# A recurrence and eight experts on one core: the second weight halves of the first two experts wait for gathered rows, and the row-number work is moved

## The chip, the cores and the metric

The kernel runs on one core of a Trainium2 chip. The metric is the device time of one execution in microseconds (us). A core has five engines with instruction streams of their own: TensorE (PE, matmuls), VectorE (DVE), ScalarE (ACT), GpSimd (POOL) and SyncE (SP, which here only issues DMAs). Each stream is executed in its written order, and the streams wait for one another, and for DMAs, on semaphores.

## The reference

A gated recurrence over 4 batches, 8 heads, 768 steps gives the rows x (3072 tokens of 384 numbers). A gate gives 8 logits for each token. Tokens are assigned greedily, by falling logit over all tokens and experts, with room for 384 tokens in each expert. Each expert then puts its 384 rows through two matrices.

```python
for t in range(S):
    state = alpha[:, :, t, :, None] * state + np.einsum('bhd,bhe->bhde', k[:, :, t], v[:, :, t])
    y[:, :, t] = np.einsum('bhd,bhde->bhe', q[:, :, t], state)
...
for idx in np.argsort(-(x @ w_gate).flatten()):
    tok, e = (int(idx) // E, int(idx) % E)
    if assigned[tok] >= 0 or counts[e] >= cap:      # cap = 3072 // 8 = 384
        continue
    assigned[tok] = e; counts[e] += 1
...
for e in range(E):
    mask = assigned == e
    out[mask] = np.maximum(x[mask] @ w1[e], 0.0) @ w2[e]   # w1[e]: 384 x 1024, w2[e]: 1024 x 384
```

## The kernel before

**First part (to about 140 us).** The recurrence is computed in chunks of 128 steps, ordered by a planner of its own. Its rows go to `x_dram`, its logits stay on the chip. The change does not touch it.

**Second part.** The experts are taken in the order in which they fill up. "Expert 0" is the first to be full, "expert 7" the last; which weights that means is known only when the search for it has ended. For every expert i the program has these steps:

- `search(i)` finds, in five rounds over the digits of the logits (`compare` on DVE, small counting matmuls `rt` on PE), which expert fills next. It ends with the number `ei` and calls `weights(i, ei)`: SP loads the raw weights `w1r` and `w2r` in two halves each (768 KB a piece). A half is `load_w1(hf)` and `load_w2(hf)`.
- `extract(i)` computes the numbers of the 384 rows: DVE builds `hot` (left operand) and `rhs` (right operand), PE multiplies them into `xt`, DVE turns that into `idx`, and POOL issues three gathers (`xr<-x_dram,idx`, 128 rows each).
- `update(i)` takes the expert's tokens out and starts the next search. It ends with the first, 3072 wide `compare` for expert i+1. It is called ahead of `search(i+1)`.
- `prep(i)`: PE transposes the three blocks of gathered rows, ACT and DVE split them into a high part `xh` and a rest `xl`.
- `split(i, hf)`: each weight half is split the same way. ACT copies the raw half into `w1hi` (rounded) and, negated, into `w1lo`; then a DMA issued by POOL adds the raw half onto the negative ("low-part DMA", `w1lo<-w1r`, `w2lo<-w2r`, function `low`), so that the rest stays. For the first half of expert 0 POOL itself subtracts `w1lo`.
- `ffn1(i, q)`, q = 0 to 7: nine matmuls into `h` (three with `xh,w1hi`, three with `xl,w1hi`, three with `xh,w1lo`); ACT makes `hh` of it and DVE `hl`. There are two `h` buffers, so that `ffn1(i, 2)` has to wait for `hh` and `hl` of `ffn1(i, 0)`.
- `ffn2(i, q)`: nine matmuls with `w2hi` and `w2lo` into the sums `y0`, `y1`, `y2`. It follows `ffn1` two steps later. At the end of an expert ACT evicts `y` to `yt`, and POOL scatters `yt` to the output (`out_dram<-yt,idx`).

Blocks q = 0 to 3 use half 0 of the weights, q = 4 to 7 half 1. There is room for two experts' raw weights.

**What sets the order.** In the second part a scheduler places the instructions of every engine at build time, by priority. The searches and row numbers of the first three experts have the highest (`ROUTE_AHEAD`). `tc.issue_after(x)` puts what is built under it behind instruction x in that order. `tc.add_manual_dep` adds a wait on the landing of a DMA. What stands in a stream is then executed strictly in that order, so that an instruction that waits holds up all that is written behind it on its engine.

The lines of before that matter here are these:

```python
half(0)                                    # L600, in weights(i, ei)
if i:
    half(1)
else:
    load_w1(1)
    second_half.append(load_w2)            # issued by extract(0), after its last gather has landed
```

Of the kernel before, what the change touches and what calls it, by code (L numbers as in the profile page):

```python
# [21 lines left out]
OP = mybir.AluOpType  # L22
# [131 lines left out]
def gla_moe_kernel(ctx, tc, q, k, v, alpha, w_gate, w1, w2, out):  # L154
    nc = tc.nc
# [29 lines left out]
    NB = CAP // 128  # L185
# [363 lines left out]
    for s in range(NS):  # L549
        pl.base = 4.4 * (NS - s)  # L550
        rows = step(s)
# [32 lines left out]
    def weights(i, ei):  # L584
        ev = nc.sync.value_load(ei[0:1, 0:1], min_val=0, max_val=E - 1)
        W1R[i] = wp.tile([128, DB, F], F32, name="w1r")
        W2R[i] = wp.tile([128, FB, Dm], F32, name="w2r")

        def load_w1(hf):
            fs = slice(hf * F // 2, (hf + 1) * F // 2)  # L590
            return nc.sync.dma_start(W1R[i][:, :, fs], w1v[bass.ds(ev, 1), :, :, fs].rearrange("e p c f -> p (e c) f"))

        def load_w2(hf):
            qs = slice(hf * FB // 2, (hf + 1) * FB // 2)
            return nc.sync.dma_start(W2R[i][:, qs], w2v[bass.ds(ev, 1), :, qs].rearrange("e p c d -> p (e c) d"))

        def half(hf):
            return load_w1(hf), load_w2(hf)

        half(0)  # L600
        if i:
            half(1)
        else:
            load_w1(1)
            second_half.append(load_w2)

    def compare(i, d, t):
        nt = 2 ** BITS[t]
# [137 lines left out]
    def update(i):  # L746
# [10 lines left out]
        if i + 2 < E:  # L757
            sg = rw.tile([128, NU], I32, name="sg")
            nc.vector.tensor_scalar(sg, m.bitcast(I32), 31, -2 ** 31, op0=OP.arith_shift_right,  # L759
                                    op1=OP.bitwise_or)  # L760
            nc.vector.scalar_tensor_tensor(asg, sel, es, asg, op0=OP.mult, op1=OP.add)
            key = rw.tile([128, NU], I32, name="key")
            nc.vector.tensor_tensor(key, m.bitcast(I32), sg, op=OP.bitwise_xor)
            val = rw.tile([128, NU, E], BF, name="val")
            nc.vector.tensor_tensor(val, lw, row(m, E), op=OP.is_equal)
            dig = rw.tile([128, nb, NU], BF, name="dig")
            digits(key, dig, rw, NU)
            st["dig"] = dig
            for _ in compare(i + 1, dig[:, 0], 0):
                pass  # L770
        else:
            nc.vector.scalar_tensor_tensor(asg, sel, es, asg, op0=OP.mult, op1=OP.add)
            val = rw.tile([128, NU, E], BF, name="val")
            nc.vector.tensor_tensor(val, lw, row(m, E), op=OP.is_equal)
# [34 lines left out]
    def extract(i):  # L809
# [15 lines left out]
        for a in range(len(halves(i, True))):  # L825
            js = halves(i, True)[a]
            x = nc.vector.tensor_tensor(words(hot, 64, js), keyed(wb, 64, js), each(iota, 64, js), op=OP.is_equal)
            if a == 0:
                nc.vector.tensor_tensor(rhs, bk, cst, op=OP.mult)
        if i < 3:  # L830
            st["hot"] = x
        ix = psx.tile([128, 2, 2, NB], F32, name="xt")
        with ExitStack() as es_:
            if i == 0:
# [13 lines left out]
        if i:  # L848
            XR[i] = wp.tile([128, NB, Dm], F32, name="xr")
        for b in range(NB):  # L850
            last_gather[0] = nc.gpsimd.indirect_dma_start(  # L851
                out=XR[i][:, b], out_offset=None, in_=x_dram,
                in_offset=bass.IndirectOffsetOnAxis(ap=IDX[i][:, b:b + 1], axis=0))

        for half in second_half:
            tc.add_manual_dep(half(1).ins, last_gather[0].ins.name,
                              mybir.DependencyInfo(mybir.DependencyClass.Sync, mybir.DependencyReason.DATA),
                              reason="rows of the first expert before its later weights")
        second_half.clear()

    last_gather = [None]

    XH, XL, CH, XA = {}, {}, {}, {}

    def split(i, hf):
# [10 lines left out]

        def low(x, raw_):
            with ExitStack() as es:
                if i == 0:
                    es.enter_context(tc.issue_after(last_gather[0].ins))  # L880
                return nc.gpsimd.dma_start(x.bitcast(F32), raw_, accum_op=OP.add, max_dma_last_dim=8192)  # L881

# [174 lines left out]
```

## Time and profile before

| | |
|---|---|
| runs | 429.5, 435.35, 435.58 us; median 435.35 us |
| the profiled execution | 426.99 us, its span (first to last instruction) 425.3 us |
| matmuls (PE) busy | 391.8 us, 92% of the span |
| DVE, ACT, POOL busy | 282.3, 214.6, 188.8 us |
| DMA | 88.05 MB, mean 207 GB/s; queue 0 (issued by POOL) 37.9%, queue 1 (issued by SP) 37.2% of 16 engines' span |
| first transpose of expert 0, 1, 2 on PE | 164.38, 196.59, 234.66 us |

Times in the profile are counted from the start of the span. A row of the timeline reads: start, duration, engine, line of the kernel, operation, output<-inputs, shape, count; in brackets follows how long the engine had been idle before it and what ended that. In a row on DMA issues the last number is the time from issue to landing in us. PEclk is the clock granted to PE, 1.00 being full.

### The profile page before, as it was taken

The numbers are of one execution on the slowest core, as the hardware profiler recorded it, in microseconds if no ns is written. First come the engines' busy times: TensorE is split into PE (matmuls) and PEld (weight loads), VectorE is DVE, ScalarE is ACT, GpSimd is POOL, SyncE is SP. The second block draws the span as 40 slices with busy tenths as digits, with TensorE's granted clock in tenths as the row PEclk, the third lists the DMA queues.
The fourth block names the chain that finished last, engine by engine and source line by source line (L and its number), as shares of the span: only waits on it lengthen the run. The fifth ranks groups of instructions, "written<-read, shape, count | busy, mean of one in ns | idle before, by whom it ended". The sixth has DMA issues, their size and how long they took to land.

```text
span 425.3 us, 10054 instructions
## 1 busy us (share of the span) xinstructions
PE 391.8 (92%) x3884; PEld 348.9 (82%) x3884; DVE 282.3 (66%) x861; ACT 214.6 (50%) x381; POOL 188.8 (44%) x206
## 2 busy tenths in 40 slices
PE   4699999999998887998998999999899999999992
PEld 1588899887886445997997898899789999999992
DVE  5999799899983585686587497796887922312210
ACT  1265655664553006526718528528626729659211
POOL 8498777766840006115505325336253342623102
PEclk9799999999999999997999699999999999999998
DMA  8967998863020149599689989998994999999701
GB/s 287 352 203 234 310 327 242 273 195 106 20 76 26 53 143 254 105 246 282 147 208 299 188 232 267 209 276 250 194 325 151 226 257 363 248 290 201 163 0 55
DMA packets 43679, 88.05 MB, mean 207 GB/s; under 512 B 3824, under 2 KB 18160, under 8 KB 43632
## 3 DMA queue, kind: packets, MB, share of 16 engines
q0 software_dynamic: 11376, 33.82, 37.9%
q1 hardware_dynamic: 32256, 53.60, 37.2%
q8 instruction: 30, 0.49, 0.5%
q14 instruction: 17, 0.14, 0.1%
HBM read 53.59 MB, written 9.44 MB: 148 GB/s over the span
## 4 chain that ended last, share of the span: by engine, by line
PE 55%; issue 14%; DVE 13%; DMA 12%; POOL 2%; ACT 1%; SPq 1%; POOLq 0%; DVEq 0%
PE h L946 15%; PE y L966 13%; DMA xr<-x_dram,idx 4%; PE y L444 4%; PE s L393 4%; PE xt L381 4%; PE y L437 4%; DMA w1lo<-w1r 4%; DMA rq<-in_q_dram 2%; PE lg L456 2%; PE rt L666 2%; PE rt L669 2%; DVE te L353 2%; PE xt L930 2%; DVE cmp L614 2%
## 5 line engine op out<-in xcount | busy, mean ns | idle before, releaser
L950 ACT ACTIVATE hh<-h 128x384 fp32r<-128x384 f32 x64 | 31.4, 490 | 94.0 <-PE h L946 93.6
L951 DVE SCALAR_TENSOR_TENSOR hl<-h,hh 128x384 fp32r<-128x384 f32 x64 | 35.4, 554 | 55.4 <-ACT hh L950 55.2
L966 PE MATMUL y<-w2hi,hh 128*128 128x384 f32 x192 | 67.6, 352 | 0.0
L966 PE MATMUL y<-w2lo,hh 128*128 128x384 f32 x192 | 67.2, 350 | 0.0
L966 PE MATMUL y<-w2hi,hl 128*128 128x384 f32 x192 | 66.6, 348 | 0.0
L977 POOL DMA_INDIRECT out_dram<-yt,idx x24 | 27.0, 1127 | 56.4 <-ACT yt L970 52.4
L881 POOL DMA_DIRECT2D w1lo<-w1r x15 | 20.2, 1346 | 67.5 <-ACT w1lo L893 55.0
L946 PE MATMUL h<-xh,w1hi 128*128 128x384 f32 x192 | 45.9, 343 | 1.7 <-DVE hl L951 1.7
L851 POOL DMA_INDIRECT xr<-x_dram,idx x24 | 29.9, 1247 | 39.3 <-DVE sg L759 18.2
L946 PE MATMUL h<-xh,w1lo 128*128 128x384 f32 x192 | 45.8, 340 | 0.0
L946 PE MATMUL h<-xl,w1hi 128*128 128x384 f32 x192 | 45.1, 339 | 0.0
L893 ACT ACTIVATE w1hi<-w1r 128x768 fp32r<-128x768 f32 x32 | 26.7, 837 | 22.5 <-DVE sg L759 21.9
L966 PEld LDWEIGHTS y<-w2hi,hh 128*128 128x128 f32 x192 | 37.5, 195 | 0.0
L363 POOL TENSOR_TENSOR kh<-rk,te 128x512 f32<-128x512 f32 (+1 forms) x24 | 29.4, 1227 | 18.0 <-DVE z L373 11.5
L966 PEld LDWEIGHTS y<-w2lo,hh 128*128 128x128 f32 x192 | 37.4, 195 | 0.0
L966 PEld LDWEIGHTS y<-w2hi,hl 128*128 128x128 f32 x192 | 37.2, 195 | 0.1
L946 PEld LDWEIGHTS h<-xh,w1hi 128*128 128x128 f32 x192 | 33.8, 189 | 2.3 <-DVE hl L951 2.0
L946 PEld LDWEIGHTS h<-xl,w1hi 128*128 128x128 f32 x192 | 34.0, 188 | 0.5 <-DVE xl L935 0.2
L946 PEld LDWEIGHTS h<-xh,w1lo 128*128 128x128 f32 x192 | 34.1, 188 | 0.0
L614 DVE TENSOR_TENSOR cmp<-nd,iota 128x1536 bf16<-128x1536 bf16 (+3 forms) x32 | 32.7, 1031 | 0.8
L396 POOL TENSOR_SCALAR_AFFINE_SELECT sm<-sm 128x1024 f32<-128x1024 f32 x24 | 26.2, 1093 | 14.1 <-ACT sm L395 12.4
L395 ACT ACTIVATE sm<-s 128x1024 f32<-128x1024 f32 x24 | 24.6, 1025 | 14.5 <-PE s L393 13.6
(182 smaller groups left out, 838.6 us busy)
## 6 DMA issues: line engine op xcount, KB each, us to landing
w1r<-in_moe_w_dram SPq DMA_DIRECT2D x16, 768.0 KB, 9.0
w2r<-in_moe_w_dram SPq DMA_DIRECT2D x16, 768.0 KB, 11.5
w2lo<-w2r POOLq DMA_DIRECT2D x16, 768.0 KB, 9.2
w1lo<-w1r POOLq DMA_DIRECT2D x15, 768.0 KB, 7.7
al<-in_alpha_dram SPq DMA_DIRECT2D x24, 260.0 KB, 4.3
rk<-in_k_dram SPq DMA_DIRECT2D x24, 256.0 KB, 4.5
rq<-in_q_dram SPq DMA_DIRECT2D x24, 256.0 KB, 4.3
rv<-in_v_dram SPq DMA_DIRECT2D x24, 192.0 KB, 3.8
```

Of the source, the lines that this page charges most:

```text
L363: eng.tensor_tensor(out_.t[:, us].rearrange("p u c -> p (u c)"), x.t[:, lo:hi], f.t[:, lo:hi], op=OP.mult)
L395: add(A_, 1.05, lambda: nc.scalar.activation(sm.t, sc.t, AF.Copy), r=[(sc, 0), (sc, 1)], w=[sm])
L396: add(G_, 1.15, lambda: nc.gpsimd.affine_select(sm.t, sm.t, pattern=[[0, 8], [1, C]], compare_op=OP.is_ge, fill=0.0, base=0, channel_multi ...
L614: nc.vector.tensor_tensor(words(dst, nt, js), keyed(d, nt, js), each(iotas[t], nt, js), op=OP.is_ge)
L851: last_gather[0] = nc.gpsimd.indirect_dma_start(out=XR[i][:, b], out_offset=None, in_=x_dram, in_offset=bass.IndirectOffsetOnAxis(ap=IDX[i ...
L881: return nc.gpsimd.dma_start(x.bitcast(F32), raw_, accum_op=OP.add, max_dma_last_dim=8192)
L893: nc.scalar.activation(dst, src, AF.Copy, scale=scale)
L946: nc.tensor.matmul(o, a[:, d], x[:, d], start=(n == 0), stop=(n == 3 * DB - 1))
L950: HA[i, q] = nc.scalar.activation(hh, o, AF.Relu)
L951: nc.vector.scalar_tensor_tensor(hl, o, 0.0, hh, op0=OP.max, op1=OP.subtract)
L966: F2[i, q] = nc.tensor.matmul(Y[b], a[:, bs], w, start=(q == 0 and n == 0), stop=(q == FB - 1 and n == 2))
L977: st_ = nc.gpsimd.indirect_dma_start(out=out, out_offset=bass.IndirectOffsetOnAxis(ap=IDX[i][:, b:b + 1], axis=0), in_=yt, in_offset=None)
```

## The change

Three things are changed. First, the second half of `w1` of expert 0, and both second halves of expert 1, are issued from `extract`, each with a wait on the landing of a gather: `w1` of expert 0 on the first of its three gathers, the others on the last. (The second half of `w2` of expert 0 waited for the last gather already.) Second, for experts 1 and 2 `rhs` is built right behind `hot` and ahead of `update`, whose start is tied to `rhs` instead of `hot`; the first `compare` for expert 3 is put behind the row numbers `idx` of expert 2. Third, the low-part DMAs of the first halves of experts 1 and 2 are put behind the gathers of that expert, as those of expert 0 are.

```diff
@@ weights
         half(0)
-        if i:
+        if i > 1:
             half(1)
         else:
-            load_w1(1)
-            second_half.append(load_w2)
+            second_half.extend((load_w1, load_w2))
@@ update
             st["dig"] = dig
-            for _ in compare(i + 1, dig[:, 0], 0):
-                pass
+            with tc.issue_after(st["idx"].ins) if i == 2 else ExitStack():
+                for _ in compare(i + 1, dig[:, 0], 0):
+                    pass
@@ extract
             if a == 0:
-                nc.vector.tensor_tensor(rhs, bk, cst, op=OP.mult)
+                with tc.issue_after(x.ins):
+                    y = nc.vector.tensor_tensor(rhs, bk, cst, op=OP.mult)
         if i < 3:
-            st["hot"] = x
+            st["hot"] = x if i == 0 else y
...
-            last_gather[0] = nc.gpsimd.indirect_dma_start(
+            gathers[b] = last_gather[0] = nc.gpsimd.indirect_dma_start(
...
-        for half in second_half:
-            tc.add_manual_dep(half(1).ins, last_gather[0].ins.name,
+        for n, load_ in enumerate(second_half):
+            tc.add_manual_dep(load_(1).ins, gathers[0 if n == i == 0 else NB - 1].ins.name,
@@ split, low
-                if i == 0:
+                if i == 0 or i < 3 and not hf:
                     es.enter_context(tc.issue_after(last_gather[0].ins))
```

Line numbers of the changed kernel differ from those of before by one in places (L966 of before is L967).

The first place is SyncE's stream around the loads of expert 1 (`w1r_2600`, `w2r_2601`; the value loaded before them is `ei`). The rows of before:

```order
L585 TENSOR_LOAD ei_2455 [waits DVE_49]
L585 ISA x2
L591 ISA
L591 DMA w1r_2600<-in_moe_w1_dram 128x3x512
L595 ISA
L595 DMA w2r_2601<-in_moe_w2_dram 128x4x384
L591 ISA
L591 DMA w1r_2600<-in_moe_w1_dram 128x3x512
L595 ISA
L595 DMA w2r_2601<-in_moe_w2_dram 128x4x384
```

In the changed kernel the second `w1r` has a wait on a DMA that POOL issued (`DMASW0`, the last gather of expert 1):

```order
L591 DMA w1r_2600<-in_moe_w1_dram 128x3x512
L595 ISA
L595 DMA w2r_2601<-in_moe_w2_dram 128x4x384
L591 ISA
L591 DMA w1r_2600<-in_moe_w1_dram 128x3x512 [waits DMASW0_49]
L595 ISA
L595 DMA w2r_2601<-in_moe_w2_dram 128x4x384
```

No row has moved; the second `w1r` waits, and with it the second `w2r` behind it. In the loads of expert 0 the second `w1r` has gained such a wait too.

The second place is ScalarE's stream where expert 1 begins. `xh_2666` are its rows, `w1hi_2804` and `w1lo_2805` its half 1, `w2lo_2807` the same of `w2`, `hh_2710` and `hh_2733` belong to `ffn1(1, 0)` and `ffn1(1, 1)`; `yt_2740` and `yt_2745` are evictions of expert 0. Before:

```order
L893 ACTIVATE w1hi_2804<-w1r_2600 128x3x256 [waits DMAHW6_49,Pool_49]
L933 ACTIVATE xh_2666<-xt_2680 128x3x128 [waits PE_49]
L970 ACTIVATE yt_2740<-y0_2279 128x384 [waits PE_49]
L970 ACTIVATE yt_2745<-y1_2280 128x384 [waits PE_49]
L893 ACTIVATE w1lo_2805<-w1r_2600 128x3x256
L893 ACTIVATE w1hi_2804<-w1r_2600 128x3x256
L893 ACTIVATE w1lo_2805<-w1r_2600 128x3x256
L950 ACTIVATE hh_2710<-h_2700 128x384 [waits DVE_49,PE_49]
L893 ACTIVATE w2lo_2807<-w2r_2601 128x768 [waits DMAHW7_49,DMASW3_49]
L950 ACTIVATE hh_2733<-h_2723 128x384 [waits DVE_49,PE_49]
```

In the changed kernel:

```order
L934 ACTIVATE xh_2666<-xt_2680 128x3x128 [waits PE_49]
L894 ACTIVATE w1hi_2804<-w1r_2600 128x3x256 [waits DMAHW6_49,Pool_49]
L971 ACTIVATE yt_2740<-y0_2279 128x384 [waits PE_49]
L894 ACTIVATE w1lo_2805<-w1r_2600 128x3x256
L894 ACTIVATE w1hi_2804<-w1r_2600 128x3x256
L894 ACTIVATE w1lo_2805<-w1r_2600 128x3x256
L951 ACTIVATE hh_2710<-h_2700 128x384 [waits DVE_49,PE_49]
L894 ACTIVATE w2lo_2807<-w2r_2601 128x768 [waits DMAHW7_49,DMASW3_49]
L951 ACTIVATE hh_2733<-h_2723 128x384 [waits DVE_49,PE_49]
```

`w1hi_2804`, which waits for the second `w1r` (`DMAHW6`), has moved behind `xh`, one eviction has moved behind `hh_2733`; `hh_2710` still stands behind the copies of half 1.

The third place is the row numbers of expert 2, on VectorE and then on GpSimd. Before, VectorE's rows (`cmp0_100` is the compare for expert 3, `other` and `idx` are the last steps to the row numbers):

```order
L782 TENSOR_TENSOR chu_3424<-ch_3421,un_3419 128x24
L783 SCALAR_TENSOR_TENSOR rem_90<-cl_3102,rem_90 128x8
L614 TENSOR_TENSOR cmp0_100<-dig_3412,iota_73 128x3072
L785 TENSOR_TENSOR o_3427<-ramp_b_75,chu_3424 128x192
L829 TENSOR_TENSOR rhs_3131<-bk_3128,cst_87 128x144
L951 SCALAR_TENSOR_TENSOR hl_2852<-h_2841,hh_2851 128x384
L676 TENSOR_TENSOR gt0_96<-rt_3431,rem_90 128x8
L842 TENSOR_SCALAR other_3148<-xt_3134 64x3
```

In the changed kernel `rhs_3131` stands 17 rows further up, right behind `hot`, and this place reads:

```order
L783 SCALAR_TENSOR_TENSOR rem_90<-cl_3102,rem_90 128x8
L843 TENSOR_SCALAR other_3148<-xt_3134 64x3
L785 TENSOR_TENSOR o_3427<-ramp_b_75,chu_3424 128x192
L844 TENSOR_SCALAR other_3148<-xt_3134 64x3
L845 TENSOR_TENSOR idx_3147<-xt_3134,other_3148 64x3
L846 TENSOR_TENSOR idx_3147<-xt_3134,other_3148 64x3
L613 TENSOR_TENSOR cmp0_100<-dig_3412,iota_73 128x3072
L952 SCALAR_TENSOR_TENSOR hl_2852<-h_2841,hh_2851 128x384
```

The four steps to `idx` now stand ahead of the compare and of one `hl`. GpSimd's rows of the same place, before (`w1lo_2805` and `w2lo_2807` are half 1 of expert 1, `w1lo_3178` and `w2lo_3180` half 0 of expert 2, `xr_3153` its gathers):

```order
L881 DMA w1lo_2805<-w1r_2600 128x3x512
L977 DMA out_0_dram<-yt_2750,idx_2152 3072x384
L881 DMA w2lo_2807<-w2r_2601 128x1536
L881 DMA w1lo_3178<-w1r_3088 128x3x512
L851 DMA xr_3153<-x_dram_62,idx_3147 128x384 x3
L881 DMA w2lo_3180<-w2r_3089 128x1536
```

In the changed kernel:

```order
L882 DMA w1lo_2805<-w1r_2600 128x3x512
L978 DMA out_0_dram<-yt_2745,idx_2151 3072x384
L978 DMA out_0_dram<-yt_2750,idx_2151 3072x384
L882 DMA w2lo_2807<-w2r_2601 128x1536
L852 DMA xr_3153<-x_dram_62,idx_3147 128x384 x3
L882 DMA w1lo_3178<-w1r_3088 128x3x512
L882 DMA w2lo_3180<-w2r_3089 128x1536
```

`w1lo_3178` has moved behind the three gathers.

More of the change, by code (lines that the diff above doesn't have):

```diff
@@ L850, in extract @@
         for b in range(NB):
-            last_gather[0] = nc.gpsimd.indirect_dma_start(
+            gathers[b] = last_gather[0] = nc.gpsimd.indirect_dma_start(
                 out=XR[i][:, b], out_offset=None, in_=x_dram,
                 in_offset=bass.IndirectOffsetOnAxis(ap=IDX[i][:, b:b + 1], axis=0))
-        for half in second_half:
-            tc.add_manual_dep(half(1).ins, last_gather[0].ins.name,
+        for n, load_ in enumerate(second_half):
+            tc.add_manual_dep(load_(1).ins, gathers[0 if n == i == 0 else NB - 1].ins.name,
                               mybir.DependencyInfo(mybir.DependencyClass.Sync, mybir.DependencyReason.DATA),
-                              reason="rows of the first expert before its later weights")
+                              reason="rows of the first experts before their later weights")
         second_half.clear()
-    last_gather = [None]
+    last_gather, gathers = [None], {}
     XH, XL, CH, XA = {}, {}, {}, {}
```

## Prediction

> **What bounds the kernel now.** I read the slices of the span first, then the second part in windows.
>
> ```profile
> PE   4699999999998887998998999999899999999992
> PEclk9799999999999999997999699999999999999998
> DMA  8967998863020149599689989998994999999701
> ```
>
> A slice is 10.6 us. PE is busy nine tenths nearly everywhere, so the time is that of PE's stream, and only what makes PE wait or run slowly can be won. Its clock drops twice in the second part, in slices 19 and 23. DMA is near its full share from slice 16 to 37, with one half empty slice (31).
>
> ```profile
> 164.00:168.00 4.00, 3.62 (x44) 3.04 (x44) 1.12 (x3) 2.42 (x5) 3.50 (x4) 1.00 1.06 184
> 196.00:205.00 9.00, 7.98 (x42) 7.15 (x42) 3.56 (x6) 4.38 (x8) 1.78 (x3) 0.62 0.99 192
> 233.00:243.00 10.00, 8.34 (x51) 7.54 (x52) 4.27 (x11) 5.27 (x9) 3.56 (x4) 0.66 0.93 197
> ```
>
> The third number from the right is the granted clock. It costs 9 x (1 - 0.62) = 3.4 us at the start of expert 1 and 10 x (1 - 0.66) = 3.4 us at that of expert 2. PE's timeline tells what it had waited for:
>
> ```profile
> 164.38 0.52 PE L930 MATMUL xt<-ident,xr 128*128 128x128 f32 x3 [3.04 <-DMA xr<-x_dram,idx]
> 166.69 0.49 PE L930 MATMUL xt<-ident,xr 128*128 128x128 f32 x3
> 196.59 0.90 PE L930 MATMUL xt<-ident,xr 128*128 128x128 f32 x3 [1.42 <-DMA xr<-x_dram,idx]
> 197.92 0.87 PE L930 MATMUL xt<-ident,xr 128*128 128x128 f32 x3 [0.43 <-DMA xr<-x_dram,idx]
> 234.66 0.90 PE L930 MATMUL xt<-ident,xr 128*128 128x128 f32 x3 [2.53 <-DMA xr<-x_dram,idx]
> ```
>
> Experts 0, 1 and 2 wait for gathered rows, 3.04, 1.85 and 2.53 us. The first wait brought no slow clock (1.00 in 164 to 168), the other two did. So there are 3.04 + (1.85 + 3.4) + (2.53 + 3.4) = 14.2 us at which the change can aim, 3.3% of the 426.99 us of the profiled execution.
>
> **Expert 0: the second `w1` half behind the first gather.** From issue to landing, in this order: that half (issued at 155.30), the first gather (158.55), the third gather of expert 2 (232.28), the quickest in this part, and the second `w2` half of expert 0 (165.25), which went beside one low-part DMA.
>
> ```profile
> w1r<-in_moe_w_dram SPq DMA_DIRECT2D x1, 768.0 KB, 8.4
> xr<-x_dram,idx POOLq DMA_INDIRECT x1, 5.7
> xr<-x_dram,idx POOLq DMA_INDIRECT x1, 3.3
> w2r<-in_moe_w_dram SPq DMA_DIRECT2D x1, 768.0 KB, 6.3
> 158.55 1.18 POOL L851 DMA_INDIRECT xr<-x_dram,idx  x1 [18.20 <-DVE sg L759]
> 161.31 1.04 POOL L851 DMA_INDIRECT xr<-x_dram,idx  x1 [0.30 <-issue]
> 167.60 0.84 ACT L893 ACTIVATE w1hi<-w1r 128x768 fp32r<-128x768 f32 x1
> 170.10 0.49 ACT L950 ACTIVATE hh<-h 128x384 fp32r<-128x384 f32 x1 [0.93 <-PE h L946]
> ```
>
> The first gather landed at 164.25, half a microsecond behind the 8.4 us load. With that load held back it should come at 158.55 + 3.3 = 161.9, the third at 161.31 + 3.3 = 164.6; PE took the third block at 166.69, so up to 2.0 us are there. The held load is then issued at 161.9 and, at 6.3 us, lands at 168.2. But its first copy, `w1hi`, stood at 167.60 on ACT, ahead of `hh` of `ffn1(0, 0)` at 170.10. From the start of that copy to `hh` ACT needs two copies (0.74 and 0.84 us apart), so `hh` starts at 169.8, only 0.3 us earlier than before, though PE is ready at 168.1. Since the two `h` buffers let one more `ffn1` run meanwhile, a part of the 2.0 us stays. I take **-1.0 us**. Bounds: -2.0 (load at 4.5 us, as the very first `w1r` alone), +1.9 (load at 8.4 us again: `hh` at 171.9). Nothing else is queued behind the waiting load on SP but the `w2` half, which waited for the third gather already.
>
> **Expert 1: both second halves behind the third gather.** These are rows of before; the DMA rows are the held `w1r` (issued 185.75), then three other `w1r` loads that went beside two low-part DMAs (issued 276.19, 328.55 and 302.32).
>
> ```profile
> w1r<-in_moe_w_dram SPq DMA_DIRECT2D x1, 768.0 KB, 9.2
> w1r<-in_moe_w_dram SPq DMA_DIRECT2D x1, 768.0 KB, 8.8
> w1r<-in_moe_w_dram SPq DMA_DIRECT2D x1, 768.0 KB, 9.8
> w1r<-in_moe_w_dram SPq DMA_DIRECT2D x1, 768.0 KB, 12.2
> w1r<-in_moe_w_dram SPq DMA_DIRECT2D x1, 768.0 KB, 4.5
> 185.75 0.43 SPq L591 DMA_DIRECT2D w1r<-in_moe_w_dram  x1
> 192.51 2.20 POOL L851 DMA_INDIRECT xr<-x_dram,idx  x1 [0.30 <-issue]
> 194.71 1.43 POOL L881 DMA_DIRECT2D w1lo<-w1r  x1
> 195.68 1.41 POOL L881 DMA_DIRECT2D w2lo<-w2r  x1
> 199.95 0.83 ACT L893 ACTIVATE w1hi<-w1r 128x768 fp32r<-128x768 f32 x1
> 204.44 0.84 ACT L893 ACTIVATE w1lo<-w1r 128x768 fp32r<-128x768 f32 x1
> 207.02 0.49 ACT L950 ACTIVATE hh<-h 128x384 fp32r<-128x384 f32 x1 [0.28 <-PE h L946]
> 203.85 0.88 PE L946 MATMUL h<-xh,w1hi 128*128 128x384 f32 x4
> 209.12 0.34 PE L946 MATMUL h<-xh,w1hi 128*128 128x384 f32 x1
> ```
>
> (The fifth is that first `w1r` of all, issued at 153.77 with nothing beside it.) *What is removed:* the gathers no longer run against four loads. They should land before PE asks, so the 1.85 us wait and the 3.4 us of slow clock go. PE would reach `ffn1(1, 2)`, at 209.12 before, at 209.12 - 1.85 - 3.4 + 0.5 (three `ffn2` matmuls that now stand ahead of it, 0.17 us each) - 1.0 (expert 0) = 203.4.
>
> *What is late instead:* the held load. The third gather took 2.20 us on POOL, ended at 194.71, and should land 2.4 us behind that end (the 3.3 us gather took 0.95 us to issue), which with the 1.0 us of expert 0 gives 196.1. Only then is `w1r` issued, beside the two low-part DMAs of half 0 that left POOL 1 to 2 us earlier. The rows of such company are 8.8, 9.8 and 12.2 us; I take 9.3, so it lands at 205.4, ten microseconds later than the 194.9 of before. ACT's `w1hi` of half 1 waits for it, and behind it in ACT's stream stand an eviction, three more copies, and `hh` of `ffn1(1, 0)`. From the landing to that `hh` it takes 0.74 + 0.39 + (207.02 - 204.44 - 0.3 of idle) = 3.4 us; `hl` on DVE is done 1.1 us later. `ffn1(1, 2)` needs that buffer, so it starts at 205.4 + 4.5 = 209.9: **+0.8 us** against before, after PE has stood still for 209.9 - 203.4 = 6.5 us. Bounds by the 4.5 and 12.2 us rows: 205.1 (-4.0) and 212.8 (+3.7). The second `w2` half lands some 3 us later, for copies that stand behind `hh`.
>
> A stall like this will bring the slow clock back, since waits of 1.85 and 2.53 us have done so: at most 3.4 us, of which a part may pass while PE still stands. I take **+3.0 us** (0 to 3.4).
>
> Here a rule bears on the price. The Trainium skill, page "TensorE: Matmul & The Clock Gate", section "HAM oscillation — how this bites in real kernels", wants no idle gap of PE above about 3.4 us. By the page a stall of 6.5 us cools the clock and one of 3 us need not; the trace does not bear out the limit, for 1.85 us cooled and 3.04 did not. By the page the sum for a stall below 3.4 us would be 3.0 us better, at 6.5 us it is the same.
>
> **Expert 2: row numbers earlier, low-part DMA behind the gathers.**
>
> ```profile
> 221.10 0.95 DVE L827 TENSOR_TENSOR hot<-wb,iota 128x1536 f16<-128x1536 bf16 x1
> 224.25 1.75 DVE L614 TENSOR_TENSOR cmp<-dig,iota 128x3072 bf16<-128x3072 bf16 x1
> 226.19 0.23 DVE L829 TENSOR_TENSOR rhs<-bk,cst 128x144 f16<-128x144 f16 x1
> 228.41 0.17 DVE L845 TENSOR_TENSOR idx<-xt,other 64x3 int32<-64x3 f32 x1
> 226.51 1.29 POOL L881 DMA_DIRECT2D w1lo<-w1r  x1 [13.46 <-ACT w1lo L893]
> 228.86 1.08 POOL L851 DMA_INDIRECT xr<-x_dram,idx  x1 [1.06 <-DVE nd L691]
> w1lo<-w1r POOLq DMA_DIRECT2D x1, 768.0 KB, 7.6
> ```
>
> `rhs` stood ready to be built at 222.1, behind `hot`, but was built at 226.19, behind the whole update and its compare. Now it costs 0.15 us there, PE multiplies during the update, and `idx` ends a little after 225, when the update's small steps end and the compare used to begin: about 3.2 us earlier. The gathers leave POOL at 225.6 instead of 228.86, and ahead of `w1lo`, whose 7.6 us ended at 234.1, half a microsecond before the first gather landed (234.61). At 3.3 to 6.7 us (the quickest, and the 189.82 to 196.54 of the first gather of expert 1 beside loads) they land from 228.9 on, at the latest at 232.3; PE asks at 234.66 - 2.53 = 232.13. The compare that moved back costs nothing: its matmuls stand behind it on PE as before. `w1lo` itself is issued near 229.5 instead of 226.51 and lands near 237; `ffn1(2, 0)` asks for it 5.9 us earlier than before, near 238, so about 1 us of cover is left. All this is counted from the same point of PE's stream and shifts with it. I take **-5.4 us** of the 5.9: half a microsecond for the second and third block. Bounds: -5.9, and 0 if the rows come later still. For expert 1 `rhs` stood right behind `hot` already, so nothing moves; its low-part DMAs already stood behind its gathers.
>
> **The sum:** +0.8 (experts 0 and 1 up to `ffn1(1, 2)`) + 3.0 - 5.4 = **-1.6 us**, that is 425.4 from the profiled 426.99. The runs shown are longer, 429.5 to 435.58, by what one trace cannot say; two further slow stretches would do. I set the difference against the mean of the four known times, 431.9, and forecast **430**. About 2% (8.6 us) is what a measurement of this kernel can tell from no change.
>
> **The rivals.**
>
> *The held loads are hidden.* If the half for expert 1 lands by 199 or so, ACT never waits: -1.0 - 4.7 - 5.6 = -11.3, 420.6. For it speaks the 4.5 us load; against it the two low-part DMAs which no edit removes, and that PE itself comes earlier.
>
> *Both held loads come late (slower).* One mechanism at two places: a held load beside low-part DMAs, ACT in front of `hh`, PE idle and cold. With the 8.4 us at expert 0 (+1.9 in place of -1.0) the +3.7 of the 12.2 us at expert 1 becomes +6.6; with the two cold stretches (3.4 each) and the gain at expert 2 it is 6.6 + 3.4 + 3.4 - 5.4 = +8.0, 440. It loses from the point at which the load of expert 1 takes over 10.5 us (landing at 206.6: 206.6 + 4.5 - 209.1 + 3.4 - 5.4 = 0).
>
> *The gathers gain nothing from the held loads.* The rows against it are the 3.3 us without and 5.7 us with loads beside. If they landed as before, the held load would leave 2.4 us later: -1.6 + 2.4 = +0.8, 433. The Trainium skill, page "DMA: Bandwidth & Descriptors", section "Queues, rings and completion order", says that a DMA engine takes its queues in turn, packet by packet. By that rule a gather of few packets would hardly wait for loads on another queue; the landing half a microsecond behind the load speaks against it here.
>
> *DMA is the bound later on.* Its share is over 0.9 in both quoted windows of experts 1 and 2, and high in the slices to 37. If transfers cannot come earlier, an earlier PE waits for them: 0, 432. Against it: slice 31 is half empty, so DMA had caught up there, and PE is not seen to wait.
>
> **How the numbers follow.** Forecast 0.45, hidden 0.25, slower 0.17, gathers without gain 0.05, DMA bound 0.08. The range goes from 418 (below the hidden case by what the slow stretches may differ) to 439, just short of the whole price of the slower one. Faster by over 2% (below 423.3) needs the hidden case nearly whole: 0.8 of 0.25 and 0.03 of the forecast, 0.23. Slower by over 2% (above 440.5) is only the end of the slower case: 0.06. Within 2%: 0.71.
>
> **What would show it.** Right: first transposes of expert 0 near 162, `w1r` of expert 1 issued near 196 and landing near 205, PE idle some 6 us before `h` released by `hl`, with a slow stretch there; no wait and a full clock at the transposes of expert 2. The forecast is wrong if that idle time is below 2 us (then it is the hidden case), or if expert 2 still waits for its rows.

## The result and the profile after

The changed kernel takes **435.16 us** (median of 20 runs, 433.19 to 436.96), the kernel before 429.9 us on the same chip. The ratio is 1.0117, 95% interval 1.0098 to 1.0135: some 5 us slower, where the prediction had said 1.6 us faster. The profiled execution took 433.19 us with a span of 431.5 us, 6.2 us more in both than the profiled execution of before.

The slices of the span, as shown of before:

```profile
PE   4799999999998888999399996999999999999992
PEclk9799999999999999999699999799999999999997
DMA  8967997853022059769688999976999999999701
```

A slice is now 10.8 us. Counted from 1, as in the prediction, PE is busy for only three tenths of slice 20 and six tenths of slice 25; the lower clock stands in slices 20 and 26. PE's timeline has the places:

```profile
162.10 0.52 PE L931 MATMUL xt<-ident,xr 128*128 128x128 f32 x3 [0.91 <-DMA xr<-x_dram,idx]
166.07 0.52 PE L931 MATMUL xt<-ident,xr 128*128 128x128 f32 x3 [1.49 <-DMA xr<-x_dram,idx]
194.43 0.85 PE L931 MATMUL xt<-ident,xr 128*128 128x128 f32 x6
212.12 0.69 PE L947 MATMUL h<-xh,w1hi 128*128 128x384 f32 x1 [8.06 <-DVE hl L952]
236.55 0.88 PE L931 MATMUL xt<-ident,xr 128*128 128x128 f32 x4
266.74 0.96 PE L665 MATMUL rt<-o,cmp 128*128 128x8 bf16 x24 [2.38 <-DVE cmp L613]
269.30 0.17 PE L683 MATMUL rt<-gt,one 128*128 128x8 bf16 x1 [0.96 <-DVE gt L675]
275.80 1.12 PE L931 MATMUL xt<-ident,xr 128*128 128x128 f32 x6
```

The waits for rows at experts 1 and 2 are gone: no bracket stands at 194.43 and 236.55. In their place there are two stalls of PE. One, of 8.06 us, is at `ffn1(1, 2)`, where the prediction had it. The other, 2.38 + 0.96 us, is at the end of expert 2, in the route's matmuls, and the prediction had nothing there. The windows around the two:

```profile
207.00:217.00 10.00, 4.88 (x23) 4.38 (x24) 2.71 (x7) 8.35 (x14) 5.39 (x5) 0.51 0.65 162
264.00:276.00 12.00, 8.66 (x63) 7.15 (x62) 6.81 (x18) 8.27 (x13) 6.95 (x7) 0.72 1.04 218
```

After each stall the granted clock (third number from the right) is low. ACT's timeline shows the same chain at both:

```profile
207.68 0.84 ACT L894 ACTIVATE w1hi<-w1r 128x768 fp32r<-128x768 f32 x1 [10.02 <-DMA w1r<-in_moe_w_dram]
210.99 0.48 ACT L951 ACTIVATE hh<-h 128x384 fp32r<-128x384 f32 x1
259.92 0.85 ACT L894 ACTIVATE w1hi<-w1r 128x768 fp32r<-128x768 f32 x1 [4.04 <-DMA w1r<-in_moe_w_dram]
262.87 0.47 ACT L951 ACTIVATE hh<-h 128x384 fp32r<-128x384 f32 x1
```

A copy of a weight half waits for its load, and `hh` stands some 3 us behind that copy in ACT's order. From `hh` on it goes through DVE: at the first place `hl`, at the second `hl` and then the compare that PE waits for.

**The account, place by place.** At `ffn1(1, 2)` PE starts at 212.12, against 209.12 before: +3.0. The slow clock that follows runs to 217.48, 5.4 us of it with PE at work, which costs 2.7. Expert 2 no longer pays its wait of 2.53 and its slow stretch of 3.4: -5.9. The three add up to -0.2, and the first matmul of `ffn1(2, 0)` does start at 241.69, against 241.88 before. Up to here the change has cost nothing. From there to the first transposes of expert 3 it loses 6.2 us: 275.80 against 269.81. The rows are first of after, then of before:

```profile
241.69 0.77 PE L947 MATMUL h<-xh,w1hi 128*128 128x384 f32 x3
...
241.88 1.05 PE L946 MATMUL h<-xh,w1hi 128*128 128x384 f32 x5
269.81 0.86 PE L930 MATMUL xt<-ident,xr 128*128 128x128 f32 x6
```

That difference stays to the end (394.08 against 387.87 for the last expert's transposes). It is 3.3 us of waits and a slow stretch of 6.8 us, 268.68 to 275.51, of which PE works 5.9 at half the clock: some 2.9 us lost.

**Why the load of expert 3 is late.** Before, `w1r` of expert 3 landed at 255.42 and ACT copied it at 255.44, without a wait. Now the copy starts at 259.92, 4.5 us later, though PE is level at `ffn1(2, 0)`. Of this, 2.5 us are a later issue and 2.0 us a longer transfer.

*The later issue.* The name of expert 3 comes out of the search, which begins behind `hot` of expert 2 (221.10 before) and ends in the issue of this load (249.93):

```profile
226.42 0.95 DVE L827 TENSOR_TENSOR hot<-wb,iota 128x1536 f16<-128x1536 bf16 x1
```

From `hot` to the load it took 28.8 us before and takes 26.0 now. PE takes 20.8 us from `hot` to `ffn1(2, 0)` before and 15.3 now, without its wait and its slow clock. So PE has won 5.5 us there and the search 2.9, and the load comes later for PE by the difference. In experiments 2, 3, 5, 6, 8, 9 and 12, where PE hardly waits for the rows of expert 2 either (0.55 us at most), the search takes 25.7 to 26.3 us.

*The longer transfer.* The loads on SP's queue and the adding DMAs on POOL's, of after:

```profile
231.08 2.45 POOL L852 DMA_INDIRECT xr<-x_dram,idx  x1 [14.50 <-PE h L947]
236.07 1.45 POOL L882 DMA_DIRECT2D w1lo<-w1r  x1
236.90 1.61 POOL L882 DMA_DIRECT2D w2lo<-w2r  x1
240.03 1.27 POOL L882 DMA_DIRECT2D w1lo<-w1r  x1 [1.53 <-ACT w1lo L894]
243.29 0.92 POOL L882 DMA_DIRECT2D w2lo<-w2r  x1
252.39 0.38 SPq L591 DMA_DIRECT2D w1r<-in_moe_w_dram  x1
```

From issue to landing, the last two of these:

```profile
w2lo<-w2r POOLq DMA_DIRECT2D x1, 768.0 KB, 12.8
w1r<-in_moe_w_dram SPq DMA_DIRECT2D x1, 768.0 KB, 7.5
```

And before, where `w1lo` of half 0 left at 226.51, ahead of the gathers, and the fourth adding DMA had landed at 251.17:

```profile
249.93 0.38 SPq L591 DMA_DIRECT2D w1r<-in_moe_w_dram  x1
...
w1r<-in_moe_w_dram SPq DMA_DIRECT2D x1, 768.0 KB, 5.5
```

Before, the four adding DMAs of expert 2 were spread from 226.5 to 251.2, and the load met 1.2 us of the last. Now all four are issued between 236.07 and 243.29, the last lands at 256.10, and the load, issued 2.5 us later itself, meets 3.7 us of it. The four begin 9.6 us later than before and end 4.9 us later.

The packets of each DMA queue (packets, MB, share of the 16 engines) show how much the load gets meanwhile. From 252.4 to 256.1 they are

```profile
q0 software_dynamic: 182, 0.79, 100.7%
```

and none of SP's queue 1; from 256.1 to 259.9 the load runs:

```profile
q1 hardware_dynamic: 639, 1.15, 84.7%
q0 software_dynamic: 40, 0.08, 10.4%
```

So the load stood behind the adding DMA that was under way. The windows of after say what filled the DMA engines earlier:

```profile
228.00:232.00 4.00, 4.00 (x29) 4.00 (x28) 3.86 (x18) 3.40 (x6) 0.92 (x1) 1.00 1.04 388
232.00:236.00 4.00, 4.00 (x44) 3.69 (x43) 2.99 (x7) 4.00 (x7) 3.40 (x3) 1.00 0.76 247
236.00:240.00 4.00, 3.96 (x47) 3.46 (x45) 2.85 (x7) 3.52 (x7) 2.50 (x3) 1.00 0.78 166
244.00:248.00 4.00, 4.00 (x33) 3.67 (x33) 2.81 (x8) 1.48 (x4) 1.25 (x2) 1.00 1.01 183
248.00:252.00 4.00, 4.00 (x33) 3.67 (x33) 2.72 (x20) 0.49 (x1) 1.00 (x1) 1.00 1.14 224
252.00:256.00 4.00, 4.00 (x26) 3.84 (x25) 4.00 (x17) 0.99 (x2) 0.00 (x0) 1.00 1.01 214
```

The last two numbers are the DMA share and GB/s. Loads alone move 388 GB/s (first row). Around the gathers a quarter of the DMA time is unused (0.76, 0.78); the adding DMAs stand behind the gathers on POOL. At 252 to 256, when the load should run, the engines are full at 214 with the adding DMA. The kernel before had as much unused time (0.77 and 0.80 from 238 to 246), but ahead of its load the engines were nearly through with the adding DMAs.

### The profile page after: what moved, and what is told of

Read it like the earlier page. It is cut to its first block, busy times and chain, and to the rows that moved or that the text cites. A ratio compares the mean times of both kernels' runs of the same rounds, so it can differ in the third digit from the quotient of the medians.

```text
span 431.5 us, 10056 instructions
## 1 busy us (share of the span) xinstructions
PE 393.2 (91%) x3884; PEld 347.9 (81%) x3884; DVE 281.9 (65%) x861; ACT 214.2 (50%) x381; POOL 187.7 (44%) x206
## 4 chain that ended last, share of the span: by engine, by line
PE 52%; DVE 15%; issue 15%; DMA 11%; ACT 3%; POOL 3%; POOLq 0%; DVEq 0%; ACTq 0%
PE h L947 13%; PE y L967 12%; DMA w1r<-in_moe_w_dram 4%; PE s L393 4%; PE y L444 4%; PE xt L381 4%; PE y L437 4%; DMA w1lo<-w1r 4%; PE lg L456 2%; DMA xr<-x_dram,idx 2%; DVE te L353 2%; PE rt L665 2%; PE rt L668 2%; DVE tp L359 2%; DVE cmp L613 2%
## 5 line engine op out<-in xcount | busy, mean ns | idle before, releaser
L967 PE MATMUL y<-w2lo,hh 128*128 128x384 f32 x192 | 67.3, 351 | 0.0
L967 PE MATMUL y<-w2hi,hh 128*128 128x384 f32 x192 | 66.8, 348 | 0.0
L967 PE MATMUL y<-w2hi,hl 128*128 128x384 f32 x192 | 65.8, 345 | 0.0
L947 PE MATMUL h<-xh,w1hi 128*128 128x384 f32 x192 | 47.5, 351 | 8.7 <-DVE hl L952 8.6
L978 POOL DMA_INDIRECT out_dram<-yt,idx x24 | 25.6, 1066 | 58.9 <-ACT yt L971 54.3
L947 PE MATMUL h<-xh,w1lo 128*128 128x384 f32 x192 | 46.8, 346 | 0.1
L967 PEld LDWEIGHTS y<-w2hi,hh 128*128 128x128 f32 x192 | 36.9, 192 | 0.3 <-ACT yt L971 0.2
L967 PEld LDWEIGHTS y<-w2lo,hh 128*128 128x128 f32 x192 | 36.9, 192 | 0.0
L967 PEld LDWEIGHTS y<-w2hi,hl 128*128 128x128 f32 x192 | 36.8, 192 | 0.1
L396 POOL TENSOR_SCALAR_AFFINE_SELECT sm<-sm 128x1024 f32<-128x1024 f32 x24 | 26.2, 1092 | 14.2 <-ACT sm L395 12.5
L395 ACT ACTIVATE sm<-s 128x1024 f32<-128x1024 f32 x24 | 24.6, 1025 | 14.5 <-PE s L393 13.6
```

What stands on the lines that cost most here:

```text
L395: add(A_, 1.05, lambda: nc.scalar.activation(sm.t, sc.t, AF.Copy), r=[(sc, 0), (sc, 1)], w=[sm])
L396: add(G_, 1.15, lambda: nc.gpsimd.affine_select(sm.t, sm.t, pattern=[[0, 8], [1, C]], compare_op=OP.is_ge, fill=0.0, base=0, channel_multi ...
L947: nc.tensor.matmul(o, a[:, d], x[:, d], start=(n == 0), stop=(n == 3 * DB - 1))
L967: F2[i, q] = nc.tensor.matmul(Y[b], a[:, bs], w, start=(q == 0 and n == 0), stop=(q == FB - 1 and n == 2))
L978: st_ = nc.gpsimd.indirect_dma_start(out=out, out_offset=bass.IndirectOffsetOnAxis(ap=IDX[i][:, b:b + 1], axis=0), in_=yt, in_offset=None)
```

## The experiments

Each was timed beside the kernel before on one chip. The diffs are shortened, and against the changed kernel unless another is named.

**1. The hold of expert 1 alone**, put into the kernel before:

```diff
-        if i:
+        if i > 1:
             half(1)
+        elif i == 0:
+            load_w1(1); second_half.append(load_w2)
         else:
-            load_w1(1); second_half.append(load_w2)
+            second_half.extend((load_w1, load_w2))
```

> The kernel of before with one edit: both second weight halves of expert 1 wait for its last gather. Theory S (the held loads are the loss): ACT waits about 10 us for the second w1 half in front of hh, PE stands still for about 8 us at ffn1(1, 2) and runs on with a slow clock (about 2.7 us lost); the wait and slow clock at the first transposes of expert 1 go (1.85 + 3.4 us), expert 2 keeps its wait of 2.5 us and slow clock. Up to ffn1(1, 2) and the slow stretch that is about +5.5 us: 435 to 437 against 430 of before. Rival N (the loss of the changed kernel is made later, behind expert 2, and the held loads cancel out): within 2 us of before.

Measured: 436.42 us, ratio 1.0117 (1.0053 to 1.018). On PE's timeline:

```profile
215.53 0.69 PE L950 MATMUL h<-xh,w1hi 128*128 128x384 f32 x1 [8.46 <-DVE hl L955]
243.25 0.55 PE L934 MATMUL xt<-ident,xr 128*128 128x128 f32 x3 [2.52 <-DMA xr<-x_dram,idx]
```

The hold by itself makes the stall, and a loss as large as that of the whole change. The wait of expert 2 for its rows is still there, and the wait at the end of expert 2 is not, so that one belongs to the other edits. This is not additive: the other edits take the 2.52 us and its slow stretch away and put the second stall in its place.

**2. All but the hold of expert 1:**

```diff
-        if i > 1:
+        if i:
             half(1)
```

> The changed kernel without the held loads of expert 1; expert 0's held load, the early row numbers and the late compare stay. Theory S: the stall at ffn1(1, 2) is gone, the transposes of expert 1 wait again 1 to 2 us with a slow clock, expert 2 has no wait: 423 to 426. Theory C (the compare that was put behind the row numbers makes the search for expert 3 late, so its weights come late and PE waits at the end of expert 2, 3.3 us and a slow clock of 3.4 us): that wait is still there, the gain of expert 2 is given back, 428 to 431. Rival R (the wait at the end of expert 2 is only an echo of the stall at expert 1): it is gone here, as under S.

Measured: 430.18 us, ratio 0.9974 (0.9938 to 1.0011). The 8 us stall is gone, and the second is not: PE, then ACT.

```profile
261.48 0.96 PE L665 MATMUL rt<-o,cmp 128*128 128x8 bf16 x24 [3.02 <-DVE cmp L613]
```

```profile
254.65 0.85 ACT L894 ACTIVATE w1hi<-w1r 128x768 fp32r<-128x768 f32 x1 [4.67 <-DMA w1r<-in_moe_w_dram]
```

So the second stall is no echo of the first. Expert 1 to expert 2 (first transposes) takes 35.0 us, 3.1 less than before; expert 2 to 3 takes 39.7, 4.5 more. What the early row numbers win is given back at once. The third edit of the diff was not run alone: beside the early row numbers it moves no instruction on any engine, since the gathers are then ahead of the adding DMAs anyway.

**3. The compare of expert 3 left ahead of `idx`:**

```diff
-            with tc.issue_after(st["idx"].ins) if i == 2 else ExitStack():
+            with ExitStack():
```

> The changed kernel with the first compare for expert 3 left where it was, ahead of the row numbers. Theory C: the loads for expert 3 leave about 2 us earlier against PE, the wait of 2.4 + 1.0 us and the slow clock at the end of expert 2 go; the gathers of expert 2 come 1.8 us later, PE waits 0 to 1 us for them: 427 to 430, with the stall at expert 1 unchanged at 8 us. Rival R: the wait at the end of expert 2 stays, 434 to 437.

Measured: 434.78 us, ratio 1.0072 (1.0035 to 1.011). Stalls of 8.14 and 3.76 us stand at the same two places, and ACT waits 4.78 us for `w1r` of expert 3. From `hot` of expert 2 to that load it takes 26.2 us, 26.0 in the changed kernel. The moved compare makes neither the second stall nor the later issue.

**4. ACT's copies of expert 1's second half behind `hh` of `ffn1(1, 1)`:**

```diff
+            if i == 1 and hf:
+                return HA[1, 1]
             return HA[i - 1, SPLIT_AFTER[i > 1]] if i and not hf else None
```

> The changed kernel with ACT's copies of expert 1's second half put behind hh of ffn1(1, 1) in ACT's order; the loads are held as before. Theory O (the order on ACT makes the loss, the load itself would be in time): no stall at ffn1(1, 2) nor after it, 427 to 430. Theory L (the held load is too late for whatever order): ffn1(1, 2) starts near 205, but the low part of w1's second half leaves POOL near 211 as before and lands near 218, so PE waits 4 to 6 us in ffn1(1, 4) instead, with a slow clock: 433 to 436.

Measured: 428.59 us, ratio 0.993 (0.9893 to 0.9967). The stall before `ffn1(1, 2)` is gone, so ACT's order made it. The time is theory O's, but its "no stall ... nor after it" did not come, nor the wait in `ffn1(1, 4)` of theory L: about half of the wait is left and has moved one step on, to PE's route.

```profile
215.81 0.57 PE L668 MATMUL rt<-o,cmp 128*128 128x16 bf16 x12 [4.54 <-DVE cmp L613]
```

```profile
213.85 0.56 DVE L954 SCALAR_TENSOR_TENSOR hl<-h,hh 128x384 fp32r<-128x384 f32 x1 [4.86 <-ACT hh L953]
```

DVE works in its written order: `hl` waits for an `hh` that stands behind the copies, and the route's steps wait behind `hl`. So late weights can stop PE before PE needs them. No stall stands at the end of expert 2 here: the DMA share stays at 0.94 or more from 226 to 254, with no thin stretch beside the gathers, and `w1r` of expert 3 lands in 4.7 us. PE also waits 1.02 us for the rows of expert 2, with a slow stretch of 3.4 us, and so comes later to that load.

**5. Without the hold of expert 1, expert 3's copies one step later on ACT** (`5 if i == 3 else SPLIT_AFTER[i > 1]` in the line above):

> The changed kernel without the hold of expert 1, and with ACT's copies of expert 3's first half placed behind hh of ffn1(2, 5), not ffn1(2, 4). Theory Q (the second loss is ACT's w1hi, which waits for the late w1r of expert 3 in front of an hh that PE needs): the load lands as late as without this edit, some 13 us behind its issue or less, but no hh stands behind the wait; PE's wait of about 3 us at the end of expert 2 goes or falls below 1 us, and with it one slow stretch: 424 to 427 us where before stands at 431. Rival T (w1r is late for PE itself, so that PE waits for expert 3's weights a few us later): 430, with a wait of PE of 2 us or more at the first ffn1 of expert 3.

Measured: 431.19 us, ratio 0.998 (0.9935 to 1.0026). As theory Q says, the stall at the end of expert 2 is gone, and expert 2 to 3 takes 33.0 us, not 39.7 as in experiment 2. But expert 3 to 4 takes 35.0, not 32.4, with a wait for an adding DMA:

```profile
277.62 0.45 PE L967 MATMUL y<-w2lo,hh 128*128 128x384 f32 x1 [1.51 <-DMA w2lo<-w2r]
```

And expert 4 to 5 takes 36.2, not 32.2, with a wait of 1.94 us for `hl` and a slow stretch of 6.8 us behind it. The kernel before waits 1.73 us at that place (308.86) and keeps its full clock, so part of what is lost there is the clock, which this wait need not have cost. Rival T has the time nearly right (430), though not the place.

**6. Without the hold of expert 1 and without one adding DMA,** `w2lo` of expert 2's first half:

```diff
-            low(lo2, w2r)
+            if (i, hf) != (2, 0):
+                low(lo2, w2r)
```

The copy that this DMA would have completed is scaled by zero, so the kernel leaves out that low part.

> The changed kernel without the hold of expert 1 and without the adding DMA of w2lo of expert 2's first half (its copy is scaled by zero, so the low part of this quarter of the expert's second weights is left out). Theory B (four adding DMAs that come late and bunched behind the gathers take the time of the loads behind them): with one of the four gone the w1r of expert 3, issued at the same place in PE's stream, lands in 5 to 6.5 us, not in 8.1; ACT's wait for it falls from 4.67 us to below 3, PE's wait at the end of expert 2 to below 1.5 us: 425 to 428 us. Rival T2 (the load is late because the route names the expert late, and takes its 8 us beside whatever runs): load 8 us, ACT's wait 4 to 5 us, PE's wait 3 us, 430 us.

Measured: 428.46 us, ratio 0.9983 (0.9951 to 1.0015). The load, issued at 249.55, lands in 5.9 us in place of 8.1, ACT waits 2.17 us in place of 4.67, PE 0.51 at the place of the 3.02. Theory B holds at its place: the adding DMAs make the load late. The time does not follow, since PE then waits for the rows of expert 3, whose gathers stand behind two adding DMAs on POOL:

```profile
271.24 1.14 PE L932 MATMUL xt<-ident,xr 128*128 128x128 f32 x6 [2.83 <-DMA xr<-x_dram,idx]
```

**7. The hold of expert 0 alone**, in the kernel before (`second_half.extend((load_w1, load_w2))` for `i == 0`, `gathers[0]` for its `w1` half and the third gather for `w2`, as in the change):

> The kernel before with the first edit for expert 0 alone (the second w1 half behind the first gather, the second w2 half behind the third). The prediction's term: the rows come 2 us earlier, 0.5 to 1.0 us of it stays, so 430.0 to 430.5 where before stands at 431, not to be told from no change within the interval; the first transposes start near 162. Rival (the held load costs more at its copies than the rows win): 432 to 434, with hh of ffn1(0, 0) behind 171.

Measured: 428.94 us, ratio 0.9982 (0.995 to 1.0015). The first transposes start at 162.52, `hh` of `ffn1(0, 0)` at 168.89, expert 1's transposes 0.2 us earlier than before. The gain of half a microsecond to one that was forecast lies within the interval: the time neither shows nor refutes it.

**8. Only the `w2` half of expert 1 held:**

```diff
-            second_half.extend((load_w1, load_w2))
+            if i == 1:
+                load_w1(1)
+                second_half.append(load_w2)
+            else:
+                second_half.extend((load_w1, load_w2))
```

> The changed kernel with expert 1's second w1 half loaded at once and only its second w2 half behind the third gather. Theory S (the stall at ffn1(1, 2) comes from the held w1r, in front of hh on ACT, and from nothing else): w1r lands near 195 as in the kernel before, the stall of 8 us is gone, since the copies of w2r stand behind the first hh; the rows of expert 1 come between those of before (195.5) and of the change (193.5), so PE waits 0 to 1.5 us for them; what is left is the second loss at the end of expert 2: 428 to 431 us. Rival (any second half that is held, w2r too, stalls ACT for PE): a stall of 4 us or more before ffn1(1, 2) or (1, 3), 433 to 436.

Measured: 430.95 us, ratio 1.0057 (1.0026 to 1.0088). At the transposes of expert 1 PE waits only 0.23 us. The time is theory S's, but S had the copies of `w2r` harmless, and that missed: one of them stands ahead of the second `hh` and waits 4.69 us, and PE loses 3.74 us and runs slowly for 6.8, near the rival's 4.

```profile
208.85 0.84 ACT L898 ACTIVATE w2lo<-w2r 128x768 fp32r<-128x768 f32 x1 [4.69 <-DMA w2r<-in_moe_w_dram]
```

**9. The changed kernel without the two adding DMAs of expert 1's first half** (as in 6, for `(1, 0)` and both; the kernel leaves out these low parts):

> The changed kernel without the two adding DMAs of expert 1's first half (their copies are scaled by zero, so the low part of half of this expert's weights is left out). Everything else, the hold included, stays. Theory S with the price from company (the held w1r of expert 1 takes 11.4 us because the adding DMAs run beside it): issued near 196 it lands in 5 to 7 us, near 202; ACT's wait for it falls from 10.0 us to about 4.5, the stall in front of ffn1(1, 2) from 8.1 to 1 to 3.5 us; 427 to 431 where before stands at 430. Rival (the load takes its 9 to 11 us by itself, since it is issued late and beside the held w2r): the stall stays at 6 us or more, 433 to 435.

Measured: 427.8 us, ratio 1.0002 (0.9968 to 1.0036). The held load, issued at 196.16, lands in

```profile
w1r<-in_moe_w_dram SPq DMA_DIRECT2D x1, 768.0 KB, 4.6
```

us in place of 11.4, and the stall falls from 8.06 us to this:

```profile
205.29 0.44 PE L948 MATMUL h<-xh,w1hi 128*128 128x384 f32 x1 [1.66 <-DVE hl L953]
```

So the price of the hold is the company of the two adding DMAs. Against the changed kernel's own ratio this is worth 1.15%, some 5 us. The stall at the end of expert 2 (2.35 us) stays, and a wait for the rows of expert 3 (1.99 us) comes to it.

**10 and 11. ACT's copies of expert 1's second half behind `hh` of `ffn1(1, 2)`** (`HA[1, 2]` in the diff of 4); in 11 the held `w1` half also waits for the first gather, not the third:

```diff
-gathers[0 if n == i == 0 else NB - 1]
+gathers[0 if n == 0 else NB - 1]
```

> The changed kernel with ACT's copies of expert 1's second half behind hh of ffn1(1, 2), one step later than in the run with them behind hh of ffn1(1, 1). Theory Q (what was left there, 4.5 us, was that hh and its hl behind the waiting copies, and DVE's steps of the route behind hl): the wait at PE falls below 2.5 us or moves to ffn1(1, 4) and is then the wait for the weights themselves, at most 4.5 us; 426 to 429. Rival (the weights are too late for PE in any order): a wait of 4.5 us or more at ffn1(1, 4), 429 to 431.

> As the run before it, and expert 1's second w1 half waits for the first gather, not the third: issued 2.7 us earlier, near 193.5. If the lateness of the weights is what is left, PE's wait gets up to 2.7 us shorter, 424 to 428; if the load then runs beside the gathers and delays the second and third block, PE waits at the transposes of expert 1 instead (1 to 2 us and a slow stretch), 428 to 431.

Measured: 430.24 us, ratio 1.0052 (1.0024 to 1.008), and **423.15 us, ratio 0.9889 (0.9848 to 0.993)**. In 10 the rival holds, with a longer wait than it says: PE gets to `ffn1(1, 4)` and waits 11.09 us for the adding DMA of the held half, which left only at 215.29, beside the loads of expert 2. In 11 the held load is issued at 194.45, ahead of the adding DMAs (196.07), and takes 4.80 us; in 10, issued at 198.01 behind them, it takes 13.59. The adding DMA then leaves at 212.70, and PE waits a quarter as long:

```profile
220.80 0.76 PE L949 MATMUL h<-xh,w1lo 128*128 128x384 f32 x3 [3.03 <-DMA w1lo<-w1r]
```

No further wait above 0.5 us stands behind it up to expert 5. The third block of rows did come late, as the other branch of the expectation has it: PE waits 1.07 us for it at 199.84, but without a slow stretch. By its ratio it beats the kernel before and the changed one.

The packets tell what company costs. In the changed kernel the held load was issued at 196.23. From 196.3 to 200.9, when the first adding DMA landed, there are 402 packets of POOL's queue 0 and none of the load; from 200.9 to 205.2, beside the second, it is this:

```profile
q0 software_dynamic: 111, 0.68, 90.5%
q1 hardware_dynamic: 107, 0.22, 15.2%
```

Only then does the load run alone. In 11 it is the other way round: from 196.1 to 198.0 the load has everything, and the adding DMA issued at 196.07 nothing:

```profile
q1 hardware_dynamic: 326, 0.67, 98.2%
```

The Trainium skill, page "DMA: Bandwidth & Descriptors", section "Queues, rings and completion order", has each DMA engine take its queues in turn, a packet at a time. The trace agrees from 200.9 to 205.2 (111 packets to 107), and not ahead of that, where the later transfer got no packet for 4.6 us.

**12. Only the `w2` half of expert 1 held (as in 8), its copies behind `hh` of `ffn1(1, 2)`:**

```diff
+            if i == 1 and hf and n > 1:
+                return HA[1, 2]
             return HA[i - 1, SPLIT_AFTER[i > 1]] if i and not hf else None
```

> Only expert 1's second w2 half is held, and its copies on ACT stand behind hh of ffn1(1, 2). In the run without the second part hh of ffn1(1, 1) stood behind the w2 copy, which waited 4.7 us, and PE stood 3.7 us and ran slowly for 6.8. Theory Q: that stall goes, 5 to 7 us at that place; what is won comes back in part as a wait at the end of expert 2 or at the rows of expert 3, since the DMA of experts 2 to 4 stays where it was (theory B): 425 to 429. Rival (nothing is given back): 423 to 425.

Measured: **423.71 us, ratio 0.9902 (0.9871 to 0.9934)**. Expert 1 to 2 takes 34.6 us (38.1 before, 42.1 in the changed kernel), at full clock. The stall at the end of expert 2 is back, 2.79 us:

```profile
261.33 0.96 PE L669 MATMUL rt<-o,cmp 128*128 128x8 bf16 x24 [2.79 <-DVE cmp L617]
```

The time stands in the rival's 423 to 425, but the kernel before was 2 us quicker here (427.68) than the 430 which the expectations of 9 name; the ratio applied to 430 gives 425.8, in theory Q's range, and the stall that Q names is there. So part of what is won is given back, and not all. By its ratio it beats both kernels too; the intervals of 11 and 12 overlap.

## Why the prediction was wrong

**Right.** Expert 0: the first transposes at 162.10 (said: near 162), the held `w1r` issued at 161.99 and landed in 6.1 us (161.9, 6.3), `hh` at 169.63 (169.8). Expert 1: no wait for rows, `w1r` issued at 196.23 (196.1), ACT's `w1hi` in front of `hh`, PE stopped by `hl`, a slow clock behind it. Expert 2: `idx` 3.1 us earlier against `hot` than before (3.2), no wait, full clock, and 5.9 us won where 5.4 were said. Two smaller misses: the third block of expert 0 came at 166.07, where the working has 164.6, and PE waited 1.49 us for it; and the gain at expert 0, said to be 1.0, was about 0.6 us at its last `hh` (192.10 against 192.69). Neither cause was tried. In the rival with hidden loads the working adds 5.6 for expert 2 where its sum takes 5.4; that moves its 420.6 by 0.2 us and nothing else.

**Mis-sized: the held load of expert 1.** The term was 9.3 us beside two adding DMAs; it took 11.4 (issued at 196.23, ACT's waiting copy at 207.68). The landing plus 4.5 us gives 212.1, where PE started. So the term of +0.8 measured +3.0, within its bounds. The working chose between rows of 8.8, 9.8 and 12.2 us, near the lower two. Experiment 9 shows that the two adding DMAs are the whole of the excess: with the held `w2r` beside it, but not them, the load takes 4.6. The prediction had named 10.5 us as the point from which it loses, and this alone would have made it +0.6 by its own sum. The slow clock came at 2.7, said 3.0.

**Missing: the load that comes behind expert 2.** The step that failed is the one that takes the 5.4 us won at expert 2 as kept: "All this is counted from the same point of PE's stream and shifts with it." On expert 2's `w1lo` it asked only whether `ffn1(2, 0)` gets it in time, and it said that the moved compare costs nothing. It did not follow the search, nor the four adding DMAs, on to the load of expert 3, nor that load's first copy in ACT's order, though that is the mechanism it had described for expert 1. That load did not shift with PE: it landed 4.5 us later against a level PE, 2.5 by its issue and 2.0 by its company. The loss there is 6.2 us, all of the measured difference. Experiment 2 shows it without the hold of expert 1. Experiment 6 shows that the adding DMAs make the transfer longer, and that with one of them less ACT still waits 2.17 us. Experiment 5 shows that ACT's order turns the late load into this stall. The rival "DMA is the bound later on", at 0.08, came nearest, and its reason against ("slice 31 is half empty, so DMA had caught up there") was weak: that slice begins at 319 us, and room there does not help a load that is due at 255.

**The clock.** The step "1.85 us cooled and 3.04 did not" stands, with more cases: 1.45 us cooled (experiment 2, at 195.79), 2.79 did not (experiment 12). At one and the same place, the first transposes of expert 0, 3.04 us did not cool before and 2.90 did in experiment 1. The 8.06 us of the changed kernel gave 10.24 us of slow clock, 5.4 of it at work. The limit near 3.4 us that the Trainium skill, page "TensorE: Matmul & The Clock Gate", section "HAM oscillation — how this bites in real kernels", gives for idle gaps is not borne out in these runs: waits below it cool the clock in some cases and not in others.

**Open.** The later issue of expert 3's load is read from the traces alone: no experiment made the search shorter, and which of its steps bound it was not tried. Nor was a kernel that puts expert 2's first adding DMA ahead of its early gathers with all else unmoved. Experiments 5 and 6 won at one place and lost at the next in one profile each; that DMA bounds the whole stretch from expert 2 to 4 is argued from that, and 11 and 12, which gain, show that it is no hard limit.

## What to carry to other kernels

When a load is held back, price it by the company it will then have: here 4.6 to 4.8 us ahead of the adding DMAs or without them, 11.4 to 13.6 behind them. Look at what stands behind its first reader on that in-order engine: moving the reader behind the work that PE needs, and issuing the load ahead of the adding DMAs, together turned a loss of 1.2% into a gain of 1.1%. When transfers are moved back, follow them to the next load that is due, not only to their own readers. And when one engine is made faster, ask whether the chain that issues its next inputs gets faster by as much: here PE won 5.5 us and the search 2.9.

## What the runs showed of the hardware

An adding DMA (768 KB, from SBUF to SBUF) takes more of the DMA engines than its size says: with such DMAs in flight the engines were full at 183 to 224 GB/s, and at 388 with loads alone. A load that was issued while one was under way got no packet until that one had landed (196.3 to 200.9 and 252.4 to 256.1 in the changed kernel); beside a second one it then took turns (200.9 to 205.2). Apart from the one that the end of the span cuts off, the slow clock came in stretches of 3.41 us (experiment 2), 6.83 (before), 10.24 (changed kernel) and 13.65 (experiment 10), whole multiples of 3.41.
